# Batch 0's attention in halves by parity, constants spread by a product, and a new order for the opening of a fused attention and FFN kernel

## The chip, the cores and the metric

One core of one Trainium2 chip runs the program. The time is device time of one execution in microseconds (us), the median of three executions. The metric is this time; lower is better.

## The reference

An attention over a small state, in both directions, feeds a feed-forward layer whose activation is a ratio of polynomials. All data are float32.

```python
# x: 8 batches, 8 heads, 512 tokens, 64; state: 8, 8, 32 slots, 64
scores = scale * x @ state^T;  a  = exp(scores - max) / (sum + 1e-9);   xread = a @ state
scores2 = scale * state @ x^T; a2 = exp(scores2 - max) / (sum + 1e-9);  sread = a2 @ x
rows = concat([xread, sread], axis=2)         # 512 + 32 rows for each of 8 batches
h = rows.reshape(4608, 512) @ w_in            # 512 -> 2048
P = a0 + a1*h + a2*h^2 + a3*h^3;  Q = 1 + |b0|*|h| + |b1|*h^2
out = (P / (Q + 1e-6)) @ w_out                # 2048 -> 512
```

The weights arrive as float64 words (two 32-bit words each) and are joined to float32 in the kernel.

## The kernel before, in words

The program is one list of tokens, `ORDER`. A loop reads it and calls one small function for each token; each engine runs its own instructions strictly in the order in which the tokens emit them. So `ORDER` sets the work order of all five engines and of the DMA queue on SP. The engines are PE (products), ACT (activations and copies out of PSUM), DVE (elementwise work), POOL (elementwise work on SBUF) and SP, which issues every transfer.

The layer runs in 72 steps n: step n is batch n // 8 with slice u = n % 8 of 256 of the 2048 hidden columns. Steps 64 to 71 do the rows of `sread` of all batches. The tokens that matter here:

- `lx`, `lr`, `ls`, `lc` (functions `load_next_x`, `load_raw`, `load_state`, `load_const`) issue transfers. Before the change the first ones stand in front of the loop, not in `ORDER`.
- `cp`, `jr`, `jl`, `js` (`conv_parts` L286, `join_rest` L292, `join_low` L305, `join_sign` L319) join one group of weight words. A group is two units of 128 x 512 words, and `jr`, `jl`, `js` run on DVE. There are 16 groups: for each u one of w_in and one of w_out. `jr` also frees two of four `raw` buffers, and the next `raw` transfers are issued there. `sp` (`conv_split` L329, L330) splits w_out's words into a high and a low part, on ACT and POOL.
- `X:i` (`extra` L573) is 32 small products on PE, state times one slice of w_in, for two batches; `XA:i` (L585) copies the result out of PSUM to an `xo` tile, of which there are two, and L587 writes it to `m_dram` in halves of 256 KB, one per batch. For batch 0 the result stays on the chip: `fh` (L595) and `fo` (L599) split it.
- `F:n` (`front` L650) is the first product of step n, in two halves; `FC`, `FB` (L662, L669), `qa`, `ln`, `ex` run on ACT, `mu`, `po`, `qd`, `g1`, `g2`, `g3` on DVE, `gl` on POOL (L713), and `mh`, `ml` are the second product into the PSUM banks o0 to o3 (L722).
- A batch's attention: `scores` (L375), `sc_copy`, then a row side (`row_T`, `row_max`, `row_sub`, `row_exp`, `row_sum`, `row_eps`, `row_norm`, `a_T`, `a_hi`, `a_lo`), whose result `aT` every `F` of the batch needs, and a column side (`col_max` to `col_norm`, `e2_T`, `e2_copy`, `sread`, `sr_copy`, `sr_T`, `sr_fin`).

All PSUM tiles other than o0 to o3 take turns in one pool with two buffers, `h`: the scores, the transposes, `ps_sr`, `ps_x` and the `h` of each step. Each new one waits until the last but one has been read.

Of the kernel before, what the change touches and what calls it, by code (L numbers as in the profile page):

```python
# [881 lines left out]
```

## Time and profile before

| what | value |
|---|---|
| median of three executions | 728.79 us (728.14 to 730.74) |
| the profiled execution, its own time | 728.87 us |
| its span, first to last instruction | 727.1 us |
| PE busy | 677.2 us (93%) |
| DVE busy | 646.6 us (89%) |
| ACT busy | 516.8 us (71%) |
| POOL busy | 309.4 us (43%) |
| mean granted clock of PE | 0.981 of 2.4 GHz |
| data moved by DMA | 81.50 MB |

The profiled execution took 0.08 us more than the median. The shares are means over the whole span: an engine that is busy 93% of it can still idle a third of one stage. A row "A <- B" under waits says what ended an engine's idle time, which need not be what began it.

### The profile page before, as it was taken

The page shows a single profiled execution, that of the slowest core. Times are in us where ns is not written, and L with a number is a line of the kernel's source. Part 1 is how long each engine was busy: PE and PEld are TensorE (multiplying, and loading weights), DVE is VectorE, ACT ScalarE, POOL GpSimd, SP SyncE. Part 2 cuts the span into 40 slices and gives each one's busy share as a digit, 9 for nine tenths or more (in the row PEclk, how much of TensorE's full clock was granted, in tenths as well). Part 3 has the DMA queues.
Part 4 walks back from the last instruction along what each step waited for, and adds up shares of the span by engine and source line. Part 5 has one row for each costly group of instructions (what it writes and reads, how often), then busy time and mean ns, then how long its engine had stood idle before and what let it go on. Part 6 is the DMA issues. An engine that isn't in the chain of part 4 may idle for free.

```text
span 727.1 us, 11661 instructions
## 1 busy us (share of the span) xinstructions
PE 677.2 (93%) x4600; PEld 525.7 (72%) x4600; DVE 646.6 (89%) x626; ACT 516.8 (71%) x636; POOL 309.4 (43%) x174
## 2 busy tenths in 40 slices
...
GB/s 258 322 277 292 252 309 232 276 161 80 96 87 43 101 60 0 102 74 115 101 60 55 92 132 28 44 116 103 15 140 54 69 0 72 61 0 59 87 1 58
DMA packets 48542, 81.50 MB, mean 112 GB/s; under 512 B 3944, under 2 KB 26600, under 8 KB 48488
## 3 DMA queue, kind: packets, MB, share of 16 engines
...
## 4 chain that ended last, share of the span: by engine, by line
PE 73%; DVE 14%; ACT 4%; issue 3%; DMA 3%; POOL 1%; SPq 0%; ACTq 0%; DVEq 0%; POOLq 0%
PE h L650 24%; PE ps_x L573 2%; DVE C L673 2%; DVE gh L694 2%; DVE A L683 2%; DVE C L677 2%; PE o__1898 L722 2%; PE o__3112 L722 2%; PE o__5554 L722 2%; PE o__3161 L722 2%; PE o__5572 L722 2%; PE o__1956 L722 2%; PE o__3182 L722 2%; PE o__6096 L722 2%; PE o__4366 L722 2%
## 5 line engine op out<-in xcount | busy, mean ns | idle before, releaser
L713 POOL TENSOR_TENSOR gl<-C,L 128x1024 fp32r<-128x1024 f32 (+1 forms) x71 | 171.7, 2419 | 243.8 <-DVE C L706 201.7
L650 PE MATMUL h<-aT,m 128*128 128x512 f32 x768 | 192.7, 396 | 2.1 <-ACT xo L585 1.0
L650 PEld LDWEIGHTS h<-aT,m 128*128 128x128 f32 x768 | 144.0, 190 | 39.3 <-ACT xo L585 3.7
L662 ACT ACTIVATE C<-h,cst 128x1024 f32<-128x1024 f32 (+1 forms) x72 | 83.2, 1155 | 60.8 <-PE h L650 36.9
L694 DVE SCALAR_TENSOR_TENSOR gh<-C,cst,L 128x1024 fp32r<-128x1024 f32 (+1 forms) x72 | 98.0, 1362 | 21.4 <-ACT L L766 4.0
L611 POOL TENSOR_TENSOR m<-m_sb,m 128x512 fp32r<-128x512 f32 x56 | 82.4, 1475 | 64.4 <-ACT m L610 45.9
L689 ACT ACTIVATE A<-A 128x1024 f32<-128x1024 f32 (+1 forms) x72 | 72.7, 1011 | 40.9 <-DVE A L683 40.9
L669 ACT ACTIVATE A<-h,cst 128x1024 f32<-128x1024 f32 (+1 forms) x72 | 76.6, 1065 | 35.3 <-PE h L650 34.7
L683 DVE SCALAR_TENSOR_TENSOR A<-A,b0a,h 128x1024 f32<-128x1024 f32 (+1 forms) x72 | 87.1, 1212 | 8.7 <-ACT C L662 6.0
L706 DVE SCALAR_TENSOR_TENSOR C<-C,cst,A 128x1024 f32<-128x1024 f32 (+1 forms) x72 | 93.1, 1293 | 1.8
L673 DVE TENSOR_TENSOR C<-C,h 128x1024 f32<-128x1024 f32 (+1 forms) x72 | 83.1, 1154 | 11.0 <-ACT C L662 5.1
L700 DVE SCALAR_TENSOR_TENSOR A<-A,gh 128x1024 f32<-128x1024 f32 (+1 forms) x72 | 89.7, 1246 | 1.7
L677 DVE SCALAR_TENSOR_TENSOR C<-C,cst,h 128x1024 f32<-128x1024 f32 (+1 forms) x72 | 87.8, 1220 | 1.9
L756 ACT ACTIVATE L<-A 128x1024 f32<-128x1024 f32 (+1 forms) x72 | 72.8, 1012 | 7.0 <-POOL gl L713 5.5
L766 ACT ACTIVATE L<-L 128x1024 f32<-128x1024 f32 (+1 forms) x72 | 72.9, 1012 | 0.9
L573 PE MATMUL ps_x<-win_sb,st 64*32 64x256 f32 x1024 | 38.7, 418 | 19.6 <-ACT xo L585 10.5
L330 POOL TENSOR_TENSOR wo<-cv_r,wo 128x512 fp32r<-128x512 f32 x16 | 23.8, 1500 | 71.7 <-ACT wo L329 71.7
L573 PEld LDWEIGHTS ps_x<-win_sb,st 64*32 64x32 f32 x1024 | 18.5, 114 | 35.7 <-ACT xo L585 13.5
L610 ACT CAST m<-m_sb 128x512 fp32r<-128x512 f32 x56 | 34.0, 611 | 1.2 <-PE h L650 1.2
L585 ACT COPY xo<-ps_x 128x1024 f32<-128x1024 f32 (+1 forms) x32 | 28.6, 903 | 8.0 <-DMA m_dram<-xo 5.7
L478 POOL TENSOR_TENSOR e<-e,rs 128x512 f32<-128x512 f32 x16 | 18.0, 1137 | 24.7 <-DVE rs L472 24.2
L650 PEld LDWEIGHTS h<-sh,m 128*128 128x128 f32 x192 | 24.2, 191 | 1.1 <-issue 0.3
...
## 6 DMA issues: line engine op xcount, KB each, us to landing
...
xT_sb<-in_xT_dram SPq DMA_DIRECT2D x16, 512.0 KB, 3.9
raw<-in_w_in_dram SPq DMA_DIRECT2D x16, 512.0 KB, 6.9
x_sb<-in_x_dram SPq DMA_DIRECT2D x16, 512.0 KB, 5.5
raw<-in_w_out_dram SPq DMA_DIRECT2D x16, 512.0 KB, 5.3
w_in_dram<-win_sb SPq DMA_DIRECT2D x8, 512.0 KB, 6.2
```

What stands on the lines that cost most here:

```text
L611: nc.gpsimd.tensor_tensor(m[:, 1], t, m[:, 0].bitcast(F32), op=ALU.subtract)
L650: nc.tensor.matmul(h[:, ci * W : (ci + 1) * W], l, r, start=(q == 0), stop=(q == len(seq) - 1),)
L662: nc.scalar.activation(e["C"], e["h"], AF.Identity, scale=cst[:, 3:4], bias=cst[:, 2:3])
L669: nc.scalar.activation(e["A"], e["h"], AF.Abs, scale=cst[:, 5:6])
L673: nc.vector.tensor_tensor(e["C"], e["C"], e["h"], op=ALU.mult)
L677: nc.vector.scalar_tensor_tensor(e["C"], e["C"], cst[:, 1:2], e["h"], op0=ALU.add, op1=ALU.mult)
L683: nc.vector.scalar_tensor_tensor(e["A"], e["A"], b0a, e["h"], op0=ALU.add, op1=ALU.mult)
L694: nc.vector.scalar_tensor_tensor(e["gh"], e["C"], cst[:, 0:1], e["L"], op0=ALU.add, op1=ALU.mult)
L700: nc.vector.scalar_tensor_tensor(e["A"], e["A"], 1.0 + 1e-6, e["gh"].bitcast(F32), op0=ALU.add, op1=ALU.mult)
L706: nc.vector.scalar_tensor_tensor(e["C"], e["C"], cst[:, 0:1], e["A"], op0=ALU.add, op1=ALU.subtract)
L713: eng.tensor_tensor(e["gl"], e["C"], e["L"], op=ALU.mult)
L722: nc.tensor.matmul(O[t], e[l][:, j * W + t * P : j * W + (t + 1) * P], wo[:, k, 2 * u + j, :], start=(u == 0 and l == "gh" and k == 0 and ...
```

## The change

It does six things.

1. Batch 0's attention runs in two halves j = 0, 1 of 512 columns: `sc_copy`, `row_T`, `row_max`, `row_sub`, `row_exp`, `row_sum`, `row_eps`, `a_T`, `a_hi`, `a_lo`, `col_max`, `col_scale`, `e2_T` and `e2_copy` each become two instructions (or groups) of half the width. Its PSUM tiles move from the pool `h` to the banks o0 to o3, which are free until the first `mh`.
2. Its `row_norm` becomes `row_norv`, on DVE instead of POOL.
3. The six constants are loaded into one partition and spread to 128 by a product with a row of ones (L241, token `cb`), and copied on ACT; before, two transfers wrote them to 128 partitions.
4. The first transfers become tokens.
5. `jl` and `js` work on one group of 1024 words in one instruction instead of two of 512.
6. `XA` of two batches writes `m_dram` with one transfer of 512 KB instead of two of 256 KB.

And `ORDER` is new from its start up to the step tokens around `F:14`; its last 1571 of 2150 tokens are as before.

```diff
-    "ls:2:8 scores:0:0 scores:0:1 sc_copy:0 col_max:0 row_T:0 col_scale:0 row_max:0 warm:8 cp:0 "
...
+    "lx:0 lr:0 cp:0 lr:1 lx:1 ls:0:2 warm:8 ls:2:8 lr:2 scores:0:0 lc cp:1 scores:0:1 lr:3 "
+    "sc_copy:0:0 jr:0 jl:0 js:0 X:0 fh:0 row_T:0:0 cp:2 sc_copy:0:1 row_T:0:1 row_max:0:0 col_max:0:0 "
...
     def load_const():
-        nc.sync.dma_start(cst[:, 0:4], ca.unsqueeze(0).broadcast_to([P, 4]))
-        nc.sync.dma_start(cst[:, 4:6], cb.unsqueeze(0).broadcast_to([P, 2]))
+        nc.sync.dma_start(cst1[:, 0:4], ca.unsqueeze(0))
+        nc.sync.dma_start(cst1[:, 4:6], cb.unsqueeze(0))
+
+    def spread_const():
+        ps = ps_o.tile([P, S], F32, name="ps_c_", tag="o3")
+        nc.tensor.matmul(ps[:, 0:6], ones, cst1, start=True, stop=True)
+        nc.scalar.copy(cst, ps[:, 0:6])
...
     def join_low(k):
-        for j in range(2):
-            y, r = CV[2 * k + j]
-            nc.vector.scalar_tensor_tensor(
-                r, y, 3, r, op0=ALU.logical_shift_left, op1=ALU.bitwise_or
-            )
+        y, r = CV[k]
+        nc.vector.scalar_tensor_tensor(
+            r, y, 3, r, op0=ALU.logical_shift_left, op1=ALU.bitwise_or
+        )
...
-    def bank(b, name):
+    def banks(b, name, o):
+        if b == 0:
+            return [
+                ps_o.tile([P, S], F32, name=f"{name}{j}_", tag=f"o{o + j}")
+                for j in range(2)
+            ]
         return ps_h.tile([P, 2, S], F32, name=name, tag="h")
...
-    def row_norm(b, j):
+    def row_norm(b, j, eng=None):
...
-        nc.gpsimd.tensor_tensor(
+        (eng or nc.gpsimd).tensor_tensor(
             e1, e1, rs.unsqueeze(2).broadcast_to([P, NT * 4, NS]), op=ALU.mult
         )
...
-        for q in range(q0, 2):
-            nc.sync.dma_start(m32[2 * e + q, u], t[:, :, q])
+        nc.sync.dma_start(
+            m32[2 * e + q0 : 2 * e + 2, u].rearrange("q p j f -> p j q f"),
+            t[:, :, q0:],
+        )
...
+        "lx": lambda i: load_next_x(),
+        "lr": lambda i: load_raw(),
+        "lc": load_const,
+        "cb": spread_const,
+        "row_norv": lambda b, j: row_norm(b, j, nc.vector),
...
     with tc.manual_schedule():
-        load_state(0, 2)
-        for _ in range(2):
-            load_next_x()
-        for _ in range(4):
-            load_raw()
-        load_const()
         for name, args in tokens:
             ops[name](*args)
```

Three places of the new order. First the DMA queue on SP at the start of the program. Before:

```order
L237 DMA st<-in_stT_dram 64x256 x2
L353 DMA xT_sb<-in_xT_dram 128x4x256 x2
L265 DMA raw<-in_w_in_dram 128x2x512 x4
L229 DMA cst<-in_ca_dram 128x4
L230 DMA cst<-in_cb_dram 128x2
L237 DMA st<-in_stT_dram 64x768 x2
```

and with the change:

```order
L366 DMA xT_sb<-in_xT_dram 128x4x256
L277 DMA raw<-in_w_in_dram 128x2x512 x2
L366 DMA xT_sb<-in_xT_dram 128x4x256
L249 DMA st<-in_stT_dram 64x256 x2
L249 DMA st<-in_stT_dram 64x768 x2
L277 DMA raw<-in_w_in_dram 128x2x512
L374 DMA x_sb<-in_x_dram 128x1024
L236 DMA cst_85<-in_ca_dram 1x4
```

The state of the first two batches, which the scores need, was the first transfer and is now behind two `xT` and two `raw`. A third `raw` follows it, and then the queue holds `x_sb`, whose buffer the first scores free.

Second, PE from the scores to the second `F` (L650, then L705). `ps_x` are the products of `X`, 16 pairs of rows each, `ps_sr` those of `sread`. Before:

```order
L375 MATMUL ps_sc<-xT_sb,st 32x256 x16
L401 MATMUL ps_s<-ident,sT 128x128 x8
L780 MATMUL warm<-ident 128x128 x8
L573 MATMUL ps_x<-win_sb,st 32x256 x32
L401 MATMUL ps_a<-ident,e_156 128x128 x8
L401 MATMUL ps_e_252<-ident,e_158 128x128 x8
L573 MATMUL ps_x<-win_sb,st 32x256 x16
L650 MATMUL h<-aT,m 128x512 x12
L573 MATMUL ps_x<-win_sb,st 32x256 x16
L508 MATMUL ps_sr<-x_sb,e2T 32x64 x32
L573 MATMUL ps_x<-win_sb,st 32x256 x16
```

and with the change, after the scores:

```order
L626 MATMUL ps_x<-win_sb,st 32x256 x16
L453 MATMUL ps_s__176<-ident,sT 128x128 x4
L453 MATMUL ps_s__177<-ident,sT 128x128 x4
L626 MATMUL ps_x<-win_sb,st 32x256 x32
L241 MATMUL ps_c__253<-cst_85,ones 128x6
L626 MATMUL ps_x<-win_sb,st 32x256 x16
L453 MATMUL ps_e__273<-ident,e_221 128x128 x4
L453 MATMUL ps_a__294<-ident,e_197 128x128 x4
L453 MATMUL ps_a__295<-ident,e_197 128x128 x4
L453 MATMUL ps_e__274<-ident,e_221 128x128 x4
L626 MATMUL ps_x<-win_sb,st 32x256 x32
L705 MATMUL h<-aT,m 128x512 x24
```

Six `X` instead of three now stand ahead of the first `F`, the second `F` follows it at once, and `sread` comes behind both.

Third, ACT just ahead of the first `F`: the copies `xo` (L638) stand between the other steps. With the change:

```order
L638 COPY xo<-ps_x 128x1024
L300 ACTIVATE cv_y<-raw 128x512
L242 COPY cst<-ps_c__253 128x6
L300 ACTIVATE cv_y<-raw 128x512
L505 COPY e2T<-ps_e__273 128x512
L466 ACTIVATE e_221,r_222<-sT,cm 128x512
L536 CAST aT<-ps_a__294 128x512
L300 ACTIVATE cv_y<-raw 128x512
L638 COPY xo<-ps_x 128x1024 x2
L536 CAST aT<-ps_a__295 128x512
```

The second part of `aT` is cast behind two `xo` copies, each of which waits for the transfer that leaves its tile.

## Rows read from the trace of the kernel before

**Rows 1.** Busy time by stretch: us, engines' busy us (instructions), PEclk, DMA share, GB/s.

```profile
0.00:27.28 27.28, 13.48 (x169) 9.46 (x169) 13.65 (x24) 12.76 (x20) 2.75 (x8) 0.94 0.82 270
...
27.28:43.16 15.88, 9.20 (x174) 5.64 (x173) 11.20 (x20) 10.99 (x18) 2.53 (x2) 0.79 0.99 330
...
56.55:147.18 90.63, 75.80 (x966) 48.20 (x967) 79.53 (x105) 69.16 (x93) 30.94 (x17) 0.94 0.80 269
147.18:219.01 71.83, 70.58 (x427) 55.27 (x427) 67.31 (x59) 55.51 (x68) 37.23 (x21) 1.00 0.31 103
```

**Rows 2.** Timeline of PE: start us, duration us, instruction, tile, [idle before it <- what ended it].

```profile
6.43 1.11 PE L375 MATMUL ps_sc<-xT_sb,st 64*32 64x256 f32 x16 [6.43 <-DMA xT_sb<-in_xT_dram]
...
10.15 1.94 PE L401 MATMUL ps_s<-ident,sT 128*128 128x128 f32 x8 [1.26 <-ACT sT L387]
...
17.31 3.72 PE L573 MATMUL ps_x<-win_sb,st 64*32 64x256 f32 x64 [2.67 <-DVE win_sb L319]
...
27.21 3.02 PE L650 MATMUL h<-aT,m 128*128 128x512 f32 x12
...
37.26 1.93 PE L508 MATMUL ps_sr<-x_sb,e2T 128*32 128x64 f32 x64 [3.73 <-issue]
...
43.16 3.02 PE L650 MATMUL h<-aT,m 128*128 128x512 f32 x12
...
56.48 2.99 PE L650 MATMUL h<-aT,m 128*128 128x512 f32 x12
...
98.41 1.96 PE L573 MATMUL ps_x<-win_sb,st 64*32 64x256 f32 x64 [0.53 <-ACT xo L585]
...
219.01 2.93 PE L650 MATMUL h<-aT,m 128*128 128x512 f32 x12
```

**Rows 3.** Waits in 0 to 160 us: who <- for whom: us in total, times, longest.

```profile
PE ps_x L573 <- ACT xo L585: 10.5, 7, 3.4
...
PE ps_sr L508 <- issue: 3.7, 1, 3.7
```

**Rows 4.** ACT groups by shape in 0 to 160 us: count, busy us, mean ns, idle before.

```profile
L585 ACT COPY xo<-ps_x 128x1024 f32<-128x1024 f32 x24 | 24.1, 1008 | 7.4 <-DMA m_dram<-xo 5.7 <-issue 1.5
...
L662 ACT ACTIVATE C<-h,cst 128x1024 f32<-128x1024 f32 x8 | 9.6, 1203 | 10.8 <-PE h L650 10.8
```

**Rows 5.** Timeline of the DMA queue on SP, its first issues.

```profile
0.74 1.24 SPq L237 DMA_DIRECT2D st<-in_stT_dram  x2
```

**Rows 6.** Busy time by stretch, as in rows 1, of the early transfers.

```profile
4.00:12.00 8.00, 4.07 (x41) 2.37 (x42) 1.39 (x2) 2.14 (x3) 0.00 (x0) 1.00 1.03 365
12.00:17.00 5.00, 2.65 (x17) 2.46 (x16) 4.84 (x9) 3.92 (x9) 0.00 (x0) 1.00 0.91 229
```

**Rows 7.** DMA issues by line: count, KB each, median us to landing.

```profile
raw<-in_w_out_dram SPq DMA_DIRECT2D x16, 512.0 KB, 5.3
w_in_dram<-win_sb SPq DMA_DIRECT2D x8, 512.0 KB, 6.2
```

**Rows 8.** The tile xo in 0 to 160 us: issues (ns min/median/max) and landing of its transfers.

```profile
L587 SPq DMA_DIRECT2D m_dram<-xo x56: 512/554/1296, 23.8 to 159.5; - x56
...
DMA to landing us min/median/max: 2.4/3.5/8.1
```

**Rows 9.** Timeline of DVE, five instructions in a row without a gap.

```profile
52.67 0.68 DVE L599 TENSOR_TENSOR m<-ps_x,m 128x512 fp32r<-128x512 f32 x1
53.27 1.28 DVE L305 SCALAR_TENSOR_TENSOR cv_r<-cv_y,cv_r 128x512 int32<-128x512 int32 x2
54.53 1.28 DVE L694 SCALAR_TENSOR_TENSOR gh<-C,cst,L 128x1024 fp32r<-128x1024 f32 x1
55.73 1.29 DVE L319 SCALAR_TENSOR_TENSOR win_sb<-cv_y,cv_r 128x512 int32<-128x512 int32 x2
56.94 1.29 DVE L319 SCALAR_TENSOR_TENSOR cv_r<-cv_y,cv_r 128x512 int32<-128x512 int32 x2
```

**Rows 10.** Timeline of POOL, batch 0's row_norm.

```profile
19.70 2.05 POOL L478 TENSOR_TENSOR e<-e,rs 128x512 f32<-128x512 f32 x2 [18.40 <-DVE rs L472]
```

More of the change, by code (lines that the diff above doesn't have):

```diff
@@ L281, in conv_parts, with join_rest @@
     def conv_parts(i):
-        raw = RAW[i]
-        y = cv.tile([P, 2 * CW], I32, name="cv_y", tag="cv", bufs=8)
-        r = cv.tile([P, 2 * CW], I32, name="cv_r", tag="cv", bufs=8)
-        CV[i] = y, r
+        k, j = divmod(i, 2)
+        if j == 0:
+            CV[k] = [
+                cv.tile([P, 2, 2 * CW], I32, name=name, tag="cv", bufs=4)
+                for name in ("cv_y", "cv_r")
+            ]
         nc.scalar.activation(
-            y.bitcast(F32), raw[:, :, 1].bitcast(F32), AF.Copy, scale=2.0**-112
+            CV[k][0][:, j].bitcast(F32),
+            RAW[i][:, :, 1].bitcast(F32),
+            AF.Copy,
+            scale=2.0**-112,
         )
-    def join_rest(k):
+    def join_rest(k, eng):
         for j in range(2):
-            nc.vector.tensor_scalar(
-                CV[2 * k + j][1],
+            eng.tensor_scalar(
+                CV[k][1][:, j],
                 RAW.pop(2 * k + j)[:, :, 0],
@@ L362, in load_next_x, with half, slots, stat @@
         X[xseq[i]] = t
-    def bank(b, name):
-        return ps_h.tile([P, 2, S], F32, name=name, tag="h")
+    def banks(b, name, o):
[3 more added lines that the diff above has]
+                for j in range(2)
+            ]
+        return ps_h.tile([P, 2, S], F32, name=name, tag="h")
+    def half(t, j):
+        if isinstance(t, list):
+            return t[j]
+        return t if j is None else t[:, j]
+    def slots(t, j):
+        t = half(t, j)
+        if j is None:
+            return t.rearrange("p j (a s) -> p (j a) s", s=NS)
+        return t.rearrange("p (a s) -> p a s", s=NS)
+    def stat(t, j):
+        return t if j is None else t[:, j * NT * 4 : (j + 1) * NT * 4]
+    def once(b, key, make):
+        T = TS[b]
+        if key not in T:
+            T[key] = make()
+        return T[key]
+    def at_tile(key, shape, bufs=None):
+        def make():
+            kw = {"bufs": bufs} if bufs else {}
+            return at.tile(shape, F32, name=key, tag=key, **kw)
+        return make
     def scores(b, g):
@@ L382, in scores, with sc_copy, col_max, col_scale @@
         load_next_x()
-    def sc_copy(b):
-        T = TS[b]
-        T["s"] = at.tile([P, 2, S], F32, name="sT", tag="sT")
-        nc.scalar.copy(T["s"], T["ps"])
-    def col_max(b):
-        T = TS[b]
-        cm = T["cm"] = at.tile([P, 2], F32, name="cm", tag="cm", bufs=2)
-        nc.vector.tensor_reduce(cm, T["s"], axis=AX.X, op=ALU.max)
-    def col_scale(b):
+    def sc_copy(b, j=None):
+        t = once(b, "sT", at_tile("sT", [P, 2, S]))
+        nc.scalar.copy(half(t, j), half(TS[b]["ps"], j))
+    def col_max(b, j=None):
+        cm = once(b, "cm", at_tile("cm", [P, 2], 2))
+        nc.vector.tensor_reduce(
+            cm if j is None else cm[:, j : j + 1],
+            half(TS[b]["sT"], j),
+            axis=AX.X,
+            op=ALU.max,
+        )
+    def col_scale(b, j=None):
         cm = TS[b]["cm"]
+        cm = cm if j is None else cm[:, j : j + 1]
         nc.vector.tensor_scalar(cm, cm, -SCALE, None, op0=ALU.mult)
-    def transposes(ps, src):
-        for j in range(2):
+    def transposes(b, key, o, src, js):
+        ps = once(b, key, lambda: banks(b, key, o))
+        for j in range(2) if js is None else (js,):
             for t in range(NT):
                 nc.tensor.transpose(
-                    ps[:, j, t * P : (t + 1) * P], src[:, j, t * P : (t + 1) * P], ident
-                )
-    def row_T(b):
-        T = TS[b]
-        T["ps"] = bank(b, "ps_s")
-        transposes(T["ps"], T["s"])
+                    half(ps, j)[:, t * P : (t + 1) * P],
+                    src[:, j, t * P : (t + 1) * P],
+                    ident,
+                )
+    def row_T(b, j=None):
+        transposes(b, "ps_s", 2, TS[b]["sT"], j)
     def col_exp(b, j):
         T = TS[b]
-        if j == 0:
-            T["e2"] = at.tile([P, 2, S], F32, name="e2", tag="e2")
-            T["r2"] = at.tile([P, 2], F32, name="r2", tag="r2", bufs=2)
+        e2 = once(b, "e2", at_tile("e2", [P, 2, S]))
+        r2 = once(b, "r2", at_tile("r2", [P, 2], 2))
         nc.scalar.activation(
-            T["e2"][:, j],
-            T["s"][:, j],
+            e2[:, j],
+            T["sT"][:, j],
             AF.Exp,
@@ L448, in col_norm @@
         nc.vector.reciprocal(r2, r2)
-    def e2_T(b):
-        T = TS[b]
-        T["ps2"] = bank(b, "ps_e2")
-        transposes(T["ps2"], T["e2"])
-    def e2_copy(b):
-        T = TS[b]
-        T["e2T"] = at.tile([P, 2, S], F32, name="e2T", tag="e2T")
-        nc.scalar.copy(T["e2T"], T["ps2"])
-    def row_exp(b):
-        e1 = TS[b]["e1"]
-        nc.scalar.activation(e1, e1, AF.Exp, scale=SCALE)
-    def row_sum(b):
-        T = TS[b]
-        rs = T["rs"] = at.tile([P, NT * 8], F32, name="rs", tag="rs", bufs=2)
-        nc.vector.tensor_reduce(rs, slots(T["e1"]), axis=AX.X, op=ALU.add)
@@ L469, in row_eps, with e2_T, e2_copy, row_exp @@
-    def row_eps(b):
-        rs = TS[b]["rs"]
+    def e2_T(b, j=None):
+        transposes(b, "ps_e2", 0, TS[b]["e2"], j)
+    def e2_copy(b, j=None):
+        t = once(b, "e2T", at_tile("e2T", [P, 2, S]))
+        nc.scalar.copy(half(t, j), half(TS[b]["ps_e2"], j))
+    def row_exp(b, j=None):
+        e1 = half(TS[b]["e1"], j)
+        nc.scalar.activation(e1, e1, AF.Exp, scale=SCALE)
+    def row_sum(b, j=None):
+        rs = once(b, "rs", at_tile("rs", [P, NT * 8], 2))
+        nc.vector.tensor_reduce(
+            stat(rs, j), slots(TS[b]["e1"], j), axis=AX.X, op=ALU.add
+        )
@@ L479, in row_norm, with a_T, a_hi @@
             e1, e1, rs.unsqueeze(2).broadcast_to([P, NT * 4, NS]), op=ALU.mult
         )
-    def a_T(b):
-        T = TS[b]
-        T["ps"] = bank(b, "ps_a")
-        transposes(T["ps"], T["e1"])
-    def a_hi(b):
-        a = AT[b] = at.tile([P, 2, 2, S], F32R, name="aT", tag="aT", bufs=2)
-        nc.scalar.copy(a[:, 0], TS[b]["ps"])
-    def a_lo(b):
+    def a_T(b, j=None):
+        transposes(b, "ps_a", 2, TS[b]["e1"], j)
+    def a_hi(b, j=None):
+        if b not in AT:
+            AT[b] = at.tile([P, 2, 2, S], F32R, name="aT", tag="aT", bufs=2)
+        nc.scalar.copy(half(AT[b][:, 0], j), half(TS[b]["ps_a"], j))
@@ L492, in a_lo @@
+    def a_lo(b, j=None):
         a = AT[b]
         nc.vector.tensor_tensor(
-            a[:, 1], TS[b]["ps"], a[:, 0].bitcast(F32), op=ALU.subtract
+            half(a[:, 1], j),
+            half(TS[b]["ps_a"], j),
+            half(a[:, 0].bitcast(F32), j),
+            op=ALU.subtract,
         )
```

71 lines of the change are left out of this document (38 added, 33 removed), and 121 rows, old and new, of the table ORDER.

## The prediction

> **What bounds the kernel now.** I read first the busy time by stretch. From 147.18 us to 219.01 us, where step 15 begins, PE is busy 70.58 of 71.83 us at full clock [rows 1, 2]: there the kernel is bound by PE, and from there on its order is as before. The opening is not. In the first 27.28 us PE is busy for 13.48 us, in the next 15.88 us for 9.20 us at a clock of 0.79 while DMA is at 0.99, and from 56.55 to 147.18 us for 75.80 of 90.63 us at 0.94, with DVE at 79.53 and DMA at 0.80 [rows 1]. No engine is full there; the steps wait for each other. What the change can gain is a part of this idle time, and what it gains by step 15 it keeps, since the work ahead of that step is the same in both.
>
> Then the timeline of PE. The first scores start at 6.43 us, when xT has landed; the first `F` at 27.21, the second at 43.16, the third at 56.48 [rows 2]. Between the first two stands a gap of 3.73 us in front of `sread` [rows 2, 3]. Its releaser reads "issue", so I looked at what its PSUM tile needs: `ps_sr` takes the buffer of the first step's `h`, which `po:0` on DVE is the last to read. The attention of batch 0 and step 0 share two buffers, and this is the place where it shows. The largest wait of PE in the opening is another one: `X` products behind `xo` copies, 10.5 us in 7 waits [rows 3], and the copies in turn wait 5.7 us for the transfers that empty their tiles [rows 4].
>
> **The change, part by part.** *The wait for the scores.* A pair of issues takes 1.24 us [rows 5], so 0.62 each. The state of batch 0 is now the fifth and sixth transfer; ahead of it and in it are 4 x 0.524 + 0.131 = 2.23 MB. From 4 us on the early transfers move at 365 GB/s [rows 6]. The first issue is a big one now, so I let them flow from 3.0 us: 3.0 + 2.23 / 0.365 = 9.1 us. The sixth issue starts at 0.74 + 5 x 0.62 = 3.8 us, and a loaded transfer of the size ahead of it lands up to 6.2 us after its issue [rows 7], so the other end is 10.0. I take 9.6: the scores start **3.2 us later** than now and end at 9.6 + 2 x 1.2 = 12.0.
>
> *The chain to the first F.* DVE joins the first weights meanwhile, so `X:0` follows the scores at once, at the slow price of 3.72 / 2 = 1.86 us [rows 2], to 13.9. The first half transpose takes 1.94 / 2 = 0.97 us [rows 2], to 14.9. From here DVE sets the pace. A pass over 512 words starts the next after 0.60 us (52.67 to 53.27), one over 1024 words after 1.20 (54.53 to 55.73) [rows 9]. Up to the two `a_lo` it has 13 passes of 512 words (two each of `row_max`, `col_max`, `row_sub`, `row_sum`, `row_norv`, `a_lo`, and `fo:0`), 7.8 us; `jr` twice, each like one such pass, 1.2; `jl:1` and `js:1`, 2.4; small ones, by the same pass each at most, some 1.2. That is 12.6, to 27.5 us. The half that waits for ACT's second copy is taken up by the `col_max` between.
>
> But `F:0` has to wait for more: its PSUM buffer is that of `X:5`, and so it waits for `XA:5`. `XA:3` ends about 20.9 (after `X:3` at 18.5, and three half-width exponentials on ACT, of some 0.8 us by my estimate from the 1.0 us of a full copy [rows 4] plus their wait). `XA:1` and `XA:2` follow the half exponential and the half cast of `aT`, at about 25.5 and 26.5. `XA:5` needs the tile of `XA:1`, so its transfer must have landed. What a merged transfer of 512 KB takes the trace does not show. Two halves take 0.55 for the second issue and 3.5 to land [rows 8], 4.1 together; a 512 KB load lands in 5.3, a 512 KB write in 6.2 [rows 7]. I take 4.7, nearer to the rows of the same tile, and keep 4.1 and 6.2. `XA:5` then ends at 25.5 + 4.7 + 0.9 = 31.1, and **F:0 starts at 31.1, 3.9 us later than now**, to 34.1. `XA:4`, by the same sum from 26.5, ends at 32.1, so `F:1` follows at once: **34.1 instead of 43.16**, 9.1 us earlier. With 6.2 for the landing both are 1.5 later, with 4.1 both 0.6 earlier.
>
> *From there to F:2.* DVE has spare work until `mu:0` can start (two passes on ACT of 1.2 us [rows 4] after `F:0`): 36.5. Then it has six step passes, 7.2 us, `jl:4`, `jr:5`, `js:4`, 3.0, and `fo:2`, 0.6: `F:2` at about 47.3 instead of 56.48, 9.2 us earlier. Not all of that is gained, for less is done by then. Counted over the two orders, DVE has 1.7 us less behind it. PE lacks three `mh` and three `ml`, 18 products like `F`'s, 12 of which take 2.93 us at full clock [rows 2], 4.4 us. What counts is 9.2 - 4.4 = 4.8 if PE feels it, 9.2 - 1.7 = 7.5 if DVE does. From 56.55 to 147.18 us both have slack [rows 1], so I take 6.3 us, about the middle.
>
> *One transfer per XA.* It saves an issue of 0.55 us [rows 8] wherever a copy waits for a landing: 5.7 us of waits [rows 4] in five places, so at most 5 x 0.55 = 2.8. The waits on the way to `F:0` are counted above. I take **0.7 more gained**, between 0 and 2.8. The bytes are the same; that it could land later is a rival.
>
> *row_norv on DVE.* Two passes of 0.60 [rows 9], and halves add a start-up each; POOL is rid of 2.05 us [rows 10], which was on the chain. The first half is in the chain above. Later DVE simply has 1.9 us more to do before step 15 (1.2 plus about 0.7 for twelve added starts). It is busy 67.31 of 71.83 us there [rows 1], so between 0 and 1.9; I take **0.6 lost**.
>
> *The joins.* Two of 512 words take from 55.73 to 56.94, 1.21 us, and one instruction of 1024 words takes 1.20 [rows 9]. 32 merged pairs gain 0.3 us at 0.01 each; `jl`'s pair takes 1.26, so its 16 gain up to 0.9 more, 1.2 at most. It is time of DVE in a stage with slack: 0. *The constants.* Nobody waits for them: they are first read behind `F:0`. In 12 to 17 us, where the old loads of many small pieces were on their way, DMA moved 229 GB/s instead of 365 at a share of 0.91 [rows 6], 1.9 us' worth. DMA is near full until 43 us [rows 1], so this may show as up to 1.9 gained; in my chain no transfer before the first `xo` decides, so 0. *The warm products* now run before anything has landed. They did not help before either: the `X` behind them took 1.86 each instead of 0.98 [rows 2]. 0.
>
> The sum: -6.3 - 0.7 + 0.6 = -6.4 us. The profiled execution took 728.87, 0.08 over the median: **722.5 us**.
>
> **A rule beside the rows.** The rows give 3.5 us to land 256 KB, 8.1 at the most [rows 8]. The Trainium skill, DMA: Bandwidth & Descriptors, section on the anatomy of one DMA, fits 2.0 us plus bytes over 436 GB/s, for another issue path than SP's. By it a merged transfer would land in about 3.2 us (an estimate from that page). No row here shows it so short at this size; the opening's queues are full.
>
> **The rivals.** *The tiles empty fast.* The quickest half in the rows landed in 2.4 us [rows 8]; with the second issue a pair takes 3.0. If a merged transfer lands in 3.0 instead of 4.7, `XA:5` ends 1.7 earlier, at 29.4, `F:0` starts then, and with it all that follows; the later waits for landing shrink too, by 5 x (4.1 - 3.0) = 5.5 at most, of which a quarter counts, as with the issues above: 722.5 - 1.7 - 1.4 = **719.4**. For it: `a_lo` is done at 27.5, so nothing else is late. Against it: DMA at 0.99 from 27 to 43 us [rows 1]. Chance 0.14. The Trainium skill's rule named above would make it this case.
>
> *The head start is given back.* Step 8 and the last joins hang on the last weight transfers, and these on four `raw` buffers that DVE frees. DVE's idle time from 56.55 to 147.18 us is 11.1 us [rows 1]; if the new order spreads as much again over the 1.9 us of added work and the 4.3 us that PE owes, of 9.2 us remain at most 9.2 - 1.9 - 4.4 = 2.9, and none if the last transfer comes no earlier. For it: DMA at 0.80 [rows 1] cannot shrink its bytes. Time 726 to 729, **727.5**. Chance 0.23.
>
> *Two xo tiles set the pace: slower.* Each `XA` holds a tile for its copy, 0.9, its issue, 0.55, and its landing L; two tiles give one `X` per (1.45 + L) / 2. There are 32; the first is ready at 13.9. Now the last `X` ends at about 146.5, just ahead of the seventh `F` (147.18). 31 x (1.45 + L) / 2 fits between up to L = 7.1 us. One in the rows took 8.1, a 512 KB write 6.2 as a median [rows 7, 8]. At L = 7.5 the chain takes 138.7 and ends at 152.6, 6.1 later: **735**. Against it: the bytes are those of two halves that were already queued together. Chance 0.13.
>
> *The change does not do what it says*: the merged joins save nothing, by the rows above; this is in the sum.
>
> **How the numbers follow.** A measurement here tells apart about 0.5%, 3.6 us. The forecast has 0.50, the fast tiles 0.14, given back 0.23, slower 0.13. So faster by over 0.5%: 0.64; within: 0.23; slower: 0.13. The range: its low end takes 7.5 for the head, 0.6 for a landing of 4.1, 2.8 for the merged issues, 1.2 for the joins and no loss, 12.1 in all, so 716.5; its high end takes in all of "given back" and the first of the slow case, 730. Less than 0.2 is left out, most of it slower.
>
> **What would show it.** Right: scores at 9 to 10 us; `F:0` at 30 to 33 and the second `F` right behind it, with no gap for `sread`; the third at 46 to 49; step 15 some 6 us before 219. Wrong: `F:0` after 34 (the landing), `F:2` near 56, or a last `raw` transfer as late as now. The forecast falls if `xo` waits for `m_dram` grow well past 5.7 us, or if step 15 stays at 219 though `F:1` came early.

## The result, and the profile after

| what | before | with the change |
|---|---|---|
| median of four executions each | 729.76 us (728.14 to 732.36) | 720.75 us (719.12 to 721.98) |
| ratio, with its 95% interval | | 0.9864 (0.9837 to 0.989) |
| the profiled execution, its span | 728.87, 727.1 us | 720.89, 719.1 us |
| PE, DVE busy | 677.2, 646.6 us | 676.1, 646.1 us |
| mean granted clock of PE | 0.981 | 0.981 |

The kernel is 9.0 us faster by the medians and 8.0 by the profiled executions; 6.4 was forecast, to 722.5, with 716.5 to 730.0 as the range. The busy time of the engines is as before, so idle time went. From step 15 to the end the two profiled executions take 508.1 and 507.8 us, at the same mean clock, so the difference lies wholly in the opening. Where in the opening is another matter. The first view is the timeline of PE after, against [rows 2].

```profile
11.93 0.60 PE L422 MATMUL ps_sc__118<-xT_sb,st 64*32 64x256 f32 x1 [6.79 <-DMA st<-in_stT_dram]
...
34.84 7.35 PE L705 MATMUL h<-aT,m 128*128 128x512 f32 x24 [3.35 <-ACT xo L638]
45.60 1.63 PE L626 MATMUL ps_x<-win_sb,st 64*32 64x256 f32 x32 [3.42 <-DVE A L738]
...
55.23 3.01 PE L705 MATMUL h<-aT,m 128*128 128x512 f32 x12 [0.39 <-ACT xo L638]
...
68.73 3.00 PE L705 MATMUL h<-aT,m 128*128 128x512 f32 x12
...
211.26 2.93 PE L705 MATMUL h<-aT,m 128*128 128x512 f32 x12
```

The scores start at 11.93 us, 5.5 us later than before. `F:0` and `F:1` follow each other without a gap, as forecast, but from 34.84, and the third `F` starts at 55.23: 1.25 us ahead of the kernel before (56.48), with 4.4 us of `mh` and `ml` still owed. In this profile the head has won nothing. Step 15 yet starts 7.75 us earlier (219.01 before), and the fourth `F` already 7.72 us (76.45 before).

So I cut both profiles at `F:0`, `F:2`, `F:4`, `F:7` and `F:15`. The columns are those of rows 1: busy us of PE, PE's weight loads, DVE, ACT, POOL, then PEclk, DMA share and GB/s. First the kernel before:

```profile
0.00:27.21 27.21, 13.41 (x168) 9.39 (x168) 13.58 (x23) 12.69 (x20) 2.75 (x8) 0.94 0.81 270
27.21:56.48 29.27, 21.11 (x340) 13.09 (x332) 24.19 (x35) 22.23 (x31) 4.94 (x3) 0.88 0.91 301
56.48:102.49 46.01, 37.26 (x454) 23.50 (x446) 39.29 (x52) 31.44 (x43) 15.52 (x8) 0.93 0.82 281
102.49:147.01 44.52, 38.44 (x519) 24.61 (x520) 40.14 (x54) 37.62 (x51) 15.43 (x9) 0.96 0.78 259
147.01:219.01 72.00, 70.75 (x428) 55.43 (x427) 67.48 (x59) 55.68 (x68) 37.23 (x21) 1.00 0.31 103
```

And the changed kernel:

```profile
0.00:34.84 34.84, 17.84 (x267) 11.69 (x267) 18.21 (x35) 17.00 (x29) 0.70 (x6) 0.85 0.86 271
34.84:55.23 20.39, 15.34 (x217) 9.89 (x217) 17.83 (x20) 15.41 (x21) 2.53 (x2) 0.75 0.90 312
55.23:89.53 34.30, 29.68 (x375) 19.82 (x376) 33.73 (x35) 28.51 (x39) 10.96 (x6) 1.00 0.93 319
89.53:142.13 52.60, 48.02 (x644) 31.73 (x642) 49.74 (x55) 43.59 (x60) 20.34 (x12) 0.97 0.80 274
142.13:211.26 69.13, 69.07 (x393) 54.84 (x394) 66.17 (x57) 54.97 (x67) 41.39 (x22) 1.00 0.31 100
```

Ahead of step 15 DVE has nearly the same work in both (184.7 and 185.7 us in these rows). Its idle time, length less busy time of each stretch, is thus a ledger that moved work does not disturb:

| DVE idle, us | to `F:0` | to `F:2` | to `F:4` | to `F:7` | to `F:15` | sum |
|---|---|---|---|---|---|---|
| before | 13.63 | 5.08 | 6.72 | 4.38 | 4.52 | 34.33 |
| with the change | 16.63 | 2.56 | 0.57 | 2.86 | 2.96 | 25.58 |
| the change's functions in the old order (below) | 11.31 | 4.39 | 2.91 | 2.13 | 4.37 | 25.11 |

The last row comes from a kernel of the experiments, cut in the same way. Its profiled execution took 720.76 us, its five others 724.4 to 725.8, so the row stands for the fastest of the six and not for their median:

```profile
0.00:23.46 23.46, 12.98 (x171) 9.24 (x171) 12.15 (x26) 11.06 (x22) 2.76 (x8) 1.00 0.83 278
23.46:53.79 30.33, 23.04 (x339) 13.55 (x332) 25.94 (x30) 23.65 (x33) 4.96 (x3) 0.83 0.92 316
53.79:96.42 42.63, 35.90 (x455) 22.71 (x447) 39.72 (x41) 31.41 (x43) 14.28 (x8) 0.96 0.87 299
96.42:139.30 42.88, 37.06 (x520) 23.93 (x520) 40.75 (x46) 37.48 (x51) 15.96 (x9) 1.00 0.83 274
139.30:211.20 71.90, 70.63 (x428) 55.39 (x427) 67.53 (x57) 55.77 (x68) 37.22 (x21) 1.00 0.32 103
```

The difference of the first two sums, 8.75, less 1.0 us more work, is the 7.75 us at step 15. Up to `F:2` the change has 19.2 us of DVE idle against 18.7. Then it loses nearly nothing: from `F:2` to `F:4` DVE is busy 33.73 of 34.30 us, where before it stood for 6.7 us. In the four other kernels of the experiments that keep this order DVE idles 0.2 to 1.3 us in that stretch.

Busy is not all work, though. One join of this stretch, the second of the pair at 59.10, lasts 2.62 us, where its like takes 0.42 as a median. While it stands, `gl` runs on POOL (DVE, then POOL):

```profile
59.10 2.96 DVE L309 TENSOR_SCALAR cv_r<-raw 128x512 int32<-128x512 uint32 x2
```

```profile
59.33 2.44 POOL L768 TENSOR_TENSOR gl<-C,L 128x1024 fp32r<-128x1024 f32 x1 [11.32 <-DVE C L761]
```

The join ends 0.3 us after `gl` (62.06 and 61.77). So some 2.2 us of the busy time are standing as well, and DVE really loses about 2.8 us in this stretch. Before, 6.7 us of idle time stand there, and some 1.4 us of the hidden kind, in two instructions at 73.89 and 75.44.

The waits of the changed kernel in 0 to 160 us: who, for whom, us in total, times, longest.

```profile
PE ps_sc__118 L422 <- DMA st<-in_stT_dram: 6.8, 1, 6.8
...
ACT xo L638 <- DMA m_dram<-xo: 5.5, 6, 1.6
PE ps_x L626 <- ACT xo L638: 4.9, 6, 1.3
```

`X` behind `xo` copies has halved (10.5 before, [rows 3]); the copies wait for their transfers as long as before (5.7, [rows 4]).

### The profile page after: what moved, and what is told of

Same layout as the page of the kernel before. It is cut to its first block, busy times and chain, and to the rows that moved or that the text cites. A ratio compares the mean times of both kernels' runs of the same rounds, so it can differ in the third digit from the quotient of the medians.

```text
span 719.1 us, 11605 instructions
## 1 busy us (share of the span) xinstructions
PE 676.1 (94%) x4602; PEld 527.7 (73%) x4602; DVE 646.1 (90%) x605; ACT 516.5 (72%) x641; POOL 309.0 (43%) x172
## 4 chain that ended last, share of the span: by engine, by line
PE 74%; DVE 12%; ACT 5%; DMA 4%; issue 2%; POOL 1%; SPq 0%; ACTq 0%; DVEq 0%; POOLq 0%
PE h L705 24%; DMA m_dram<-xo 3%; PE ps_x L626 3%; DVE C L728 2%; DVE A L738 2%; DVE gh L749 2%; PE o__1880 L777 2%; PE o__1823 L777 2%; PE o__3047 L777 2%; DVE C L732 2%; PE o__1899 L777 2%; PE o__3096 L777 2%; PE o__5489 L777 2%; PE o__5507 L777 2%; PE o__5463 L777 2%
## 5 line engine op out<-in xcount | busy, mean ns | idle before, releaser
L768 POOL TENSOR_TENSOR gl<-C,L 128x1024 fp32r<-128x1024 f32 (+1 forms) x71 | 173.8, 2448 | 271.0 <-DVE C L761 209.4
L705 PE MATMUL h<-aT,m 128*128 128x512 f32 x768 | 193.8, 398 | 4.8 <-ACT xo L638 3.7
L705 PEld LDWEIGHTS h<-aT,m 128*128 128x128 f32 x768 | 145.2, 191 | 40.4 <-ACT xo L638 5.1
L343 POOL TENSOR_TENSOR wo<-cv_r,wo 128x512 fp32r<-128x512 f32 x16 | 22.1, 1401 | 61.9 <-ACT wo L342 61.9
L638 ACT COPY xo<-ps_x 128x1024 f32<-128x1024 f32 (+1 forms) x32 | 28.8, 906 | 9.2 <-DMA m_dram<-xo 5.5
L300 ACT ACTIVATE cv_y<-raw 128x512 f32<-128x512 f32 x32 | 21.3, 685 | 8.0 <-DMA raw<-in_w_in_dram 7.6
L705 PEld LDWEIGHTS h<-sh,m 128*128 128x128 f32 x192 | 24.3, 191 | 1.1 <-issue 0.3
```

The lines of the kernel that those rows point to most:

```text
L705: nc.tensor.matmul(h[:, ci * W : (ci + 1) * W], l, r, start=(q == 0), stop=(q == len(seq) - 1),)
L768: eng.tensor_tensor(e["gl"], e["C"], e["L"], op=ALU.mult)
```

## The experiments

Three theories stood first. **H**: the head makes the gain. **M**: the new order behind `F:2` makes it. **W**: the merged write does. Later ones were a theory G or "filler", that products kept back fill PE's gap behind `F:2`, and A, that the halves and their banks do it. Each ratio is to the kernel before on the same chip.

### The merged write, taken out and put in alone

```diff
-        nc.sync.dma_start(
-            m32[2 * e + q0 : 2 * e + 2, u].rearrange("q p j f -> p j q f"),
-            t[:, :, q0:],
-        )
+        for q in range(q0, 2):
+            nc.sync.dma_start(m32[2 * e + q, u], t[:, :, q])
```

In the changed kernel: 

> The changed kernel with each xo written to m_dram in two transfers of 256 KB again; all else, the order too, as in the change. Theory W (the merged write frees the xo tiles sooner, and that is the gain of 8 us between the third and the eighth F): back by 5 us or more, 725 to 728 us, ratio to the kernel before 0.993 to 0.998, and ACT's wait for m_dram grows from 5.5 us to over 10. Theory H (the gain is the head: batch 0's halves, its own PSUM banks, the second F right behind the first) and theory M (the gain is the order between the third F and the eighth, which keeps DVE supplied): within 1.5 us of the change, 719.5 to 722.5, ratio 0.986 to 0.990; the prediction's own term for this was 0.7.

Measured 721.04 us, ratio 0.986 (0.9814 to 0.9907). The reverse edit in the kernel before: 

> The kernel before with the merged write alone. Theory W: 721 to 724 us, ratio 0.989 to 0.993. Theories H and M: 727 to 730, ratio 0.997 to 1.001.

Measured 731.1 us, ratio 0.9992 (0.9974 to 1.001). ACT's wait for `m_dram` was 6.2 us in the first of the two, not over 10. W falls in both: the write is worth nothing that shows.

### New head with the old rest, and old head with the new rest

```diff
 ORDER, the new one up to the 164th token
-X:10 sr_T:0 F:3:0 F:3:1 sr_fin:0 qa:2 ln:2 g2:1 XA:10 mh:0:0 jl:6 ...
+X:10 sr_T:0 sr_fin:0 mh:0:0 ml:0:0 jl:6 g2:1 js:6 qa:2 ln:2 XA:10 mh:1:2 ...
```

> The changed kernel's functions and its order up to the first F:3 token; all tokens that are left then follow in the order of the kernel before. Theory H: 720 to 723 us, ratio 0.986 to 0.992. Theory M: the middle loses its supply again, 725 to 730, ratio 0.994 to 1.002, with DVE near 84% busy between F:3 and F:7 instead of 93%. Theory W: 721 to 723, since the writes are merged.

Measured 728.24 us, ratio 0.9971 (0.9944 to 0.9998). In its profile `F:2` starts at 53.38, `F:3` at 71.64, 4.8 us ahead of the kernel before, and `F:4` at 101.50, 1.0 ahead. The lead goes where the old order goes on. H falls as the whole cause. M had the time but not its sign: between `F:3` and `F:7` DVE is busy 67.73 of 74.08 us, 91% and not 84%. Up to step 15 DVE idles 28.5 us here, 5.8 less than before, but it is busy for 189.2 us, 4.5 more: between `F:2` and `F:4` alone four of its instructions last 1.0 to 2.2 us longer than their like, each beside one on POOL. Most of the idle time that went came back as longer instructions.

```diff
 ORDER, the old one up to F:2:0; batch 0 in full width, in the pool h
-X:7 cp:12 cp:13 js:5 sp:11 F:2:0 F:2:1 jr:6 FC:2 ...
+X:7 cp:12 cp:13 js:5 sp:11 X:12 F:2:0 fh:3 F:2:1 XA:12 jr:6 FB:2 FC:2 ...
...
-        if b == 0:
+        if b < 0:
```

> The changed kernel's functions, but batch 0's attention in full width and in the shared pool of two PSUM buffers, and the order of the kernel before (with its first transfers in the old order) up to the first F:2 token; the tokens that are left follow in the order of the change. Theory H: 726 to 730 us, ratio 0.995 to 1.002. Theory M: 719 to 723, ratio 0.986 to 0.992, with DVE at 90% or more between F:2 and F:7. Theory W: 721 to 724.

Measured 736.38 us, ratio 1.0068 (1.004 to 1.0095). The timeline of PE of this kernel, at its third `F`:

```profile
66.10 5.04 PE L703 MATMUL h<-aT,m 128*128 128x512 f32 x12 [5.56 <-DVE m L652]
```

All three theories missed the time. The stall is at the seam, where the new order asks for `X:12` and `m` that the old head had not prepared. So M as a part by itself falls, but this run says little of its size: an order written by hand does not come apart at one token.

### The state first

```diff
-lx:0 lr:0 cp:0 lr:1 lx:1 ls:0:2 warm:8 ls:2:8 lr:2 scores:0:0 lc cp:1 scores:0:1 lr:3
+ls:0:2 lx:0 lr:0 cp:0 lr:1 lx:1 warm:8 ls:2:8 lr:2 lr:3 scores:0:0 lc cp:1 scores:0:1
```

> The changed kernel, with the two state transfers of batch 0 issued first and the third raw-and-on transfer (lr:3) issued ahead of the scores instead of behind them. In the changed kernel the scores waited to 11.93 us because st, issued at 2.80, landed 8.99 us later behind 2 MB. Both theories expect the scores at 6.5 to 8.5 us. Theory H (the head's lead counts): F:0 comes 2 to 4 us earlier (31 to 33), F:2 follows by as much, and the time falls by 2 to 4 us to about 717 to 719. Theory G (only what is won between F:2 and F:3 counts, a lead ahead of F:2 is given back while PE and DVE wait for weights): F:2 stays within 1.5 us of 55.2 and the time within 1.5 us of 720.9.

Measured 721.14 us, ratio 0.9865 (0.9843 to 0.9888); `F:0` at 35.35, `F:2` at 55.75. Neither theory had the scores right. Their first half started at 5.93, the second at 12.97. The chains of waits show it, the changed kernel and then this one (start us, us, what):

```profile
2.80 8.99 DMA st<-in_stT_dram
```

```profile
3.71 9.21 DMA xT_sb<-in_xT_dram
```

The wait moved from `st` to the second `xT`: whichever input of the scores was issued behind the first two `raw` transfers landed some 9 us later in these two profiles. As `F:0` did not come earlier, H was not put to the test here.

### row_norm back on POOL

```diff
-row_norv:0:0 e2_copy:0:0 row_norv:0:1
+row_norm:0:0 e2_copy:0:0 row_norm:0:1
```

> The changed kernel with batch 0's row_norm back on POOL (two halves). The prediction counted 0.6 us lost for the move to DVE, between 0 and 1.9. If DVE's added work counts, this kernel gains 0.6 to 1.9 us (719 to 720.3). If the chain to F:0 counts, POOL's halves (about 1.0 us each, after a hand-over each way) instead of 0.6 delay aT by 0.5 to 1.5 us; F:0 itself hung on XA:5 (33.77), not on a_lo (32.1), so F:0 moves by under 0.5 us and the time stays within 0.5 us of the changed kernel.

Measured 722.71 us, ratio 0.9872 (0.9849 to 0.9896): no gain, and no loss outside the interval. `F:0` came at 35.22.

### Filler: step 0's second products behind F:2, in the kernel before

```diff
-mh:0:2 cp:10 FC:1 X:8 mh:0:3 g3:0 ... mh:0:0 ln:1 fo:2 gl:0 jl:5 ex:1 g1:1 ml:0:2 ml:0:0 ml:0:3 X:6 ... F:2:0 F:2:1 jr:6
+cp:10 FC:1 X:8 g3:0 ... ln:1 fo:2 gl:0 jl:5 ex:1 g1:1 X:6 ... F:2:0 F:2:1 mh:0:2 mh:0:3 mh:0:0 ml:0:2 ml:0:0 ml:0:3 jr:6
```

> The kernel before, in which only six tokens of step 0's second product (mh:0:2, mh:0:3, mh:0:0, ml:0:2, ml:0:0, ml:0:3; mh:0:1 and ml:0:1 already stood there) are moved from ahead of F:2 to right behind it, as the changed kernel has them. Before, PE lost 9.8 us between F:2 (56.48) and F:3 (76.45); with the change 3.3. Theory G, filler: the kept products fill that gap, F:2 comes up to 4 us earlier and F:3 follows; the time falls by 2 to 4 us to 727 to 729. Rival (the gap is set by the one PSUM buffer and by the landing of m_dram, not by missing work for PE): F:2 comes earlier, F:3 stays at 76 to 77 us and the time within 1 us of before (731).

Measured 732.88 us, ratio 1.0021 (1.0004 to 1.0039); `F:2` at 58.68, `F:3` at 79.06. The interval from `F:2` to `F:3` is 20.4 us, 20.0 before. Filler falls: the 18 products fit into the gap, but `F:2` came no earlier without them, and the `X` ahead of `F:3` waits as before for an `xo` copy (3.30 us, 3.38 before). The rival's figures, `F:3` at 76 to 77 and a time within 1 us, were missed as well. The run also shows how far two profiles of one program part: up to `F:1` its tokens are those of the kernel before, and `F:0` starts at 28.37 instead of 27.21. Single starts are read to about 1.5 us here at best; the last experiment has one that parts by over 2.

### The change's functions in the old order

```diff
-sc_copy:0 col_max:0 row_T:0 col_scale:0 row_max:0 warm:8 cp:0 ...
+sc_copy:0:0 sc_copy:0:1 col_max:0:0 col_max:0:1 row_T:0:0 row_T:0:1 col_scale:0:0 ...
```

> All of the change's functions (halves for batch 0, PSUM banks o0 to o3 for them, row_norm on DVE, spread constants, joins of 1024 words, merged writes) under the order of the kernel before, each split token followed by its second half in the same place. Theory O (the order is what gains): the functions alone give at most 2 us, 729 to 732; sread no longer waits for po:0, so the 3.7 us gap ahead of it shrinks to under 1, and F:1 moves up by up to 3, but the lead is gone by F:3. Rival B (the borrowed banks gain by themselves): F:1 near 40 and the time at 726 or less.

Measured 725.1 us (720.76 to 725.76, six runs), ratio 0.9904 (0.988 to 0.9928). The expectation names row_norm on DVE; the old order's tokens keep it on POOL, so it is not in this run. Theory O falls: the functions alone give over half of the gain, 5.5 us by the medians, and the order is not needed for that. Rival B had the figures (`F:1` at 39.71, a time under 726) but not the path: the lead was there at `F:0` already and grew again later, and that the banks gain by themselves is what the next runs deny. Timeline of PE of this kernel:

```profile
23.46 3.18 PE L705 MATMUL h<-aT,m 128*128 128x512 f32 x12
29.79 1.96 PE L626 MATMUL ps_x<-win_sb,st 64*32 64x256 f32 x32 [3.15 <-ACT xo L638]
...
35.45 1.96 PE L626 MATMUL ps_x<-win_sb,st 64*32 64x256 f32 x32 [1.83 <-DVE C L732]
...
39.71 3.01 PE L705 MATMUL h<-aT,m 128*128 128x512 f32 x12
...
71.29 1.10 PE L626 MATMUL ps_x<-win_sb,st 64*32 64x256 f32 x32 [1.17 <-DVE m L654]
72.32 3.02 PE L705 MATMUL h<-aT,m 128*128 128x512 f32 x12
```

`F:0` is 3.75 us earlier. `F:1` is 3.45 earlier, so the interval between them is 16.25 us, 15.95 before: `sread` waits for nothing now, but the `X` behind it waits for the same buffers that step 0 holds (1.83 <- DVE C). The 3.73 us of [rows 3] were, by this, a wait that passed on to the next user.

### Which functions

Three kernels in the old order. The first with all of the change's functions, but batch 0 in full width and in the shared pool:

```diff
-sc_copy:0:0 sc_copy:0:1 col_max:0:0 col_max:0:1 row_T:0:0 row_T:0:1 ...
+sc_copy:0 col_max:0 row_T:0 ...
...
-        if b == 0:
+        if b < 0:
```

> All functions of the change under the order of the kernel before, as in the run banks_old_order (725.1 us, F:0 at 23.46, F:1 at 39.71, F:3 at 72.32 in its profile), but batch 0's attention in full width and in the shared pool h again: what is left are the spread constants, the joins of 1024 words and the merged writes. Theory A (halves and borrowed banks make the gain): the gain goes, F:0 returns to 26.5 to 27.5, F:1 to 42 to 43.5 and the time to 729 to 732. Rival (joins and constants make it): F:0 as in the kernel before, but the lead grows over the joins from F:1 to F:7 and the time is at 725 to 727.

Measured 729.21 us, ratio 0.9977 (0.9961 to 0.9994); `F:0` at 29.00, `F:1` at 44.89. The second with halves and banks alone:

```diff
-        nc.sync.dma_start(cst1[:, 0:4], ca.unsqueeze(0))
+        nc.sync.dma_start(cst[:, 0:4], ca.unsqueeze(0).broadcast_to([P, 4]))
...
-        y, r = CV[k]
+        for j in range(2):
+            y, r = (t[:, j] for t in CV[k])
...
+        for q in range(q0, 2):
+            nc.sync.dma_start(m32[2 * e + q, u], t[:, :, q])
```

> The reverse: old order, batch 0 in halves in the borrowed banks, and everything else as in the kernel before (joins of 512 words, constants by two broadcast transfers, two writes per XA). Theory A: nearly all of the gain stays, F:0 at 23 to 24.5, F:1 at 39 to 40.5, time 723 to 727. Rival (joins and constants): 729 to 732; between the two, 727 to 729, if both have a share.

Measured 729.42 us, ratio 0.9983 (0.9966 to 0.9999). The third with all functions and halves, but in the pool:

```diff
-        if b == 0:
+        if b < 0:
```

> Old order, all functions of the change, batch 0 in halves, but its PSUM tiles in the shared pool h. It tells halves from banks. If the halves make the gain (each engine starts on half of the work while the one before does the other): F:0 at 23.5 to 25, F:1 about 16 us behind, time 725 to 727. If the banks make it (no wait for the buffer of a step's h ahead of sread, 3.7 us before): F:0 at 26 to 27.5, F:1 at 42 to 43.5, time 729 to 731; with both, F:0 early and F:1 at 41 to 42, 727 to 728.

Measured 729.97 us, ratio 0.9986 (0.9962 to 1.0009). Timeline of PE of the third, and below it of the second:

```profile
22.87 1.94 PE L453 MATMUL ps_a<-ident,e 128*128 128x128 f32 x8 [1.92 <-issue]
...
29.28 4.16 PE L705 MATMUL h<-aT,m 128*128 128x512 f32 x12
...
40.46 1.94 PE L558 MATMUL ps_sr<-x_sb,e2T 128*32 128x64 f32 x64 [3.73 <-issue]
```

```profile
24.82 3.56 PE L712 MATMUL h<-aT,m 128*128 128x512 f32 x12
...
41.39 3.71 PE L712 MATMUL h<-aT,m 128*128 128x512 f32 x12
...
73.94 1.96 PE L635 MATMUL ps_x<-win_sb,st 64*32 64x256 f32 x32 [3.68 <-ACT xo L647]
75.83 3.54 PE L712 MATMUL h<-aT,m 128*128 128x512 f32 x12
```

The profile of the third is of an execution of 733.03 us and that of the second of one of 727.33, so their starts compare only roughly. Halves without banks do not bring `F:0` forward (29.28). The transposes and `sread` stand there for 1.92 and 3.73 us with "issue" as the releaser, which I read, as the prediction did, as a wait for the shared buffers. Banks and halves do bring it forward (24.82), and of that lead at `F:0`, 2.4 us, 0.6 is left at `F:3` (75.83 against 76.45), less than single starts can tell. There an `X` waits 3.68 us for an `xo` copy; with the other functions too it waits 1.17, for `m`. So A is half right: without halves and banks the gain goes, but alone they do not bring it. The parts do not add: 0.2% for halves in banks, 0.2% for the rest, and 1.0% together. That was measured on two chips, each kernel beside its own runs of the kernel before; with their errors taken as independent the two parts make 0.63% at most, and the whole makes 0.72% at least. **Which of constants, joins and writes keeps the lead was not told apart.** Row_norm, which is on POOL in all of these, has no part in it.

### Narrow joins in the changed kernel

```diff
-        y, r = CV[k]
-        nc.vector.scalar_tensor_tensor(
-            r, y, 3, r, op0=ALU.logical_shift_left, op1=ALU.bitwise_or
-        )
+        for j in range(2):
+            y, r = (t[:, j] for t in CV[k])
+            nc.vector.scalar_tensor_tensor(
+                r, y, 3, r, op0=ALU.logical_shift_left, op1=ALU.bitwise_or
+            )
```

and the same for `js`. 

> The changed kernel with jl and js in two instructions of 512 words again, nothing else. The prediction counted the wider joins at nothing (0 to 1.2 us), as time of DVE in a stage with slack. In the profile of the changed kernel DVE has no slack there: 33.73 of 34.30 us busy from 55.23 to 89.53, and a join of 1024 words starts the next instruction after 1.13 to 1.15 us, where two of 512 took 1.21. Theory D (DVE bounds the stage now, so each saved start-up counts): 32 joins by 0.07 are 2.2 us, so the time rises by 1.5 to 2.6 us, to 722.4 to 723.5. As the prediction had it: within 0.7 us of the changed kernel (720.2 to 721.6).

Measured 718.99 us (717.77 to 720.43), ratio 0.9821 (0.9808 to 0.9835). Theory D falls as a forecast of the time: narrow joins are no slower, and this is the fastest kernel of the study. Against the changed kernel's ratio the intervals just part, but the two were measured on different chips, each beside its own runs of the kernel before, and never side by side. The profile of this kernel gives a reason to be careful. The joins do cost DVE more; a pair starts the next instruction after 1.20 us, the wide join after 1.13 (DVE timelines, this kernel and then the changed one):

```profile
46.18 1.29 DVE L322 SCALAR_TENSOR_TENSOR cv_r<-cv_y,cv_r 128x512 int32<-128x512 int32 x2
47.38 0.79 DVE L309 TENSOR_SCALAR cv_r<-raw 128x512 int32<-128x512 uint32 x2
```

```profile
49.02 1.22 DVE L321 SCALAR_TENSOR_TENSOR cv_r<-cv_y,cv_r 128x1024 int32<-128x1024 int32 x1
50.15 0.76 DVE L309 TENSOR_SCALAR cv_r<-raw 128x512 int32<-128x512 uint32 x2
```

But its head was earlier, and from before the first join. The chain of waits of this kernel:

```profile
2.81 6.75 DMA st<-in_stT_dram
```

`st` landed after 6.75 us instead of 8.99, with the same transfers ahead of it; the scores started at 9.70 and `F:0` at 32.10, 2.7 us ahead of the changed kernel. At `F:4` 0.45 of it is left (89.08 against 89.53), at step 15 0.32 (210.94). The profiled execution took 720.43 us, the longest of the five; the shorter ones have no profile. What the joins are worth by themselves stays open.

## Why the prediction was right, and where it was not

The time, the sign and the range held. The path did not: by the prediction's own last part, `F:0` after 34 and `F:2` near 56 were to show it wrong, and they came at 34.84 and 55.23.

*The wait for the scores* was put at 9.6 us, 10.0 at most. It was 11.93, as `st` landed 8.99 us after its issue. The step that failed is the rate, the bytes ahead over 365 GB/s: from 4 to 12 us DMA moved 276 GB/s here, at a share of 1.02, where the kernel before moved 365 at 1.03 [rows 6]. In the kernel with narrow joins, where `st` landed after 6.75 us, it moved 312. Why the rate fell the runs do not show. The other end, 10.0, took the 6.2 us of [rows 7] for the most that a transfer takes; it is a median.

*The chain to the first F* was right in kind. The timeline of ACT after, the copies that were named:

```profile
28.40 1.93 ACT L638 COPY xo<-ps_x 128x1024 f32<-128x1024 f32 x2
...
33.77 1.01 ACT L638 COPY xo<-ps_x 128x1024 f32<-128x1024 f32 x1 [1.00 <-DMA m_dram<-xo]
```

`XA:5` did release `F:0`. It waited for the transfer of `XA:1` and ended at 34.78 instead of 31.1. `XA:1`, the first of the two copies at 28.40, was done at about 29.4 and not at 25.5: 2.3 us of that are the scores, the rest ACT's waits for `raw` words ahead of it. Its transfer, issued at 29.44, had landed by 33.77, a little under the 4.7 taken. The page after gives it as a median, and the tile's answer with its spread:

```profile
m_dram<-xo SPq DMA_DIRECT2D x24, 512.0 KB, 4.4
```

```profile
DMA to landing us min/median/max: 2.6/4.5/9.8
```

The Trainium skill, DMA: Bandwidth & Descriptors, section on the anatomy of one DMA, has a fit for another issue path than SP's that would make this 3.2 us, an estimate from that page. The measured 4.4 decides, and with it the rival of tiles that empty fast fell.

*From there to F:2*, the term of 6.3 us, is the step that failed. `F:2` was put at 47.3 and came at 55.23. Of these 7.9 us, 3.7 are the late `F:0`. Another 1.5 lie between `F:0` and `mu:0`, 6.9 us and not 5.4: the 12 products of `F:0` took 4.62 us, where those of `F:2` take 3.01 at full clock. From 34.84 to 42.19, over both `F`, the granted clock was 0.77, so in part at 1.2 GHz, the lower of its two levels, after PE had stood for 3.35 us. The last 2.7 lie between `mu:0` and `F:2`, 13.5 us and not 10.8 (DVE, then two pieces of the chain of waits):

```profile
41.73 1.22 DVE L728 TENSOR_TENSOR C<-C,h 128x1024 f32<-128x1024 f32 x1 [1.45 <-ACT C L717]
...
52.41 0.69 DVE L654 TENSOR_TENSOR m<-ps_x,m 128x512 fp32r<-128x512 f32 x1 [0.37 <-ACT xo L638]
```

```profile
34.84 4.62 PE h L705 x12
...
54.27 0.90 ACT xo L638
```

DVE was done with `fo:2` at 53.0, 11.3 us after `mu:0`, nearly as counted. But the prediction let `F:2` follow `fo:2` at once, and `F:2` takes the PSUM buffer of `X:6`: it waited for `XA:6`, a copy that stood on ACT behind `ex:0` and ended at 55.17. That wait, 2.2 us, is not in the sum. It is not one odd profile: in the six kernels that have the new head `F:0` came at 32.10 to 35.63 and `F:2` at 51.64 to 56.63.

The head gained nothing by DVE's ledger. What the prediction held to be slack that would stay as it is, "From 56.55 to 147.18 us both have slack", is what the change took: 6.15 us of DVE idle between `F:2` and `F:4` (some 5.4 with the hidden standing of both kernels counted in), 1.5 to `F:7`, 1.6 to step 15. A term of nearly the right size stood in the wrong stretch, so the sum came out by luck as much as by working.

*The smaller terms.* One transfer per `XA`: 0.7 counted, nothing shown, within its bounds. *row_norv*: 0.6 lost was counted; back on POOL it is no faster. *Joins* at 0: open, as the run with narrow joins could not tell. *Constants* at 0: open, since they may have a share in what keeps the halves' lead.

*The rivals.* "Given back" had the head right, and its conclusion wrong: the head start was gone at `F:2`, but DVE's later idle time shrank where the rival let it grow, and the last `raw` transfers were issued at 123.5 us instead of 132.0. Something like it did happen in the new head with the old rest, 728.24 where 727.5 was put. "Two xo tiles set the pace" fell: the waits for `m_dram` stayed at 5.5 us.

*What the cause is.* Shown: the functions without the new order give 0.96%; with batch 0 in full width 0.23%, with its halves in the pool 0.14%, with an interval that takes in no gain, and the halves in their banks alone 0.17%; the new head with the old rest 0.29%; all together 1.36%. Shown too: in the changed kernel DVE hardly idles from `F:2` on. On the chip of the functions in the old order (0.9904) two kernels with the new order had 0.9865 and 0.9872, so the order adds some 0.3 to 0.4%, by intervals that still overlap. Argued, not shown: that the order does this by setting joins and steps so that DVE always has one of them ready. The old functions in the new order were not tried, nor was the new order with batch 0's halves in the shared pool.
